# Twenty first-layer units ahead of pairs 8 and 9 in a fused attention and feed-forward kernel

## The chip, the cores and the metric

The kernel runs on one core of one Trainium2 chip. A core has TensorE (PE, matrix products into PSUM), VectorE (DVE), ScalarE (ACT), GpSimd (POOL) and SyncE (SP); SP here does nothing but issue DMAs, and POOL issues DMAs beside its copies. Each engine runs its instructions in the order of the program, and waits for other engines by semaphores. The metric is the device time of one execution in microseconds; the median of several executions counts.

## What is computed

Sliding-window attention with global rows, and behind it two dense layers with the activation h·cos(h):

```python
def _attn_ref(q, k, v, global_idx):            # (8, 8, 576, 64)
    scores = scale * np.matmul(q, k.transpose(0, 1, 3, 2))
    mask = np.abs(pos[:, None] - pos[None, :]) <= 32
    mask = mask | is_global[:, None] | is_global[None, :]
    attn = softmax(np.where(mask, scores, -1e9))
    return np.matmul(attn, v)
def _moe_ref(x, w_in, w_out):                  # (4608, 512), (512, 2048), (2048, 512)
    h = x @ w_in
    g = h * np.cos(h)
    return g @ w_out
```

The eight heads of a batch entry stand side by side in the 512 columns of x; 8 × 576 tokens give 4608 rows.

## The kernel before

**Attention** goes by pairs of heads: 32 pairs, four to a batch entry. A pair's 576 tokens are cut into 11 blocks of 56 queries; to each block belong 8 global columns and a window of 120 keys. The steps of one pair `pr`:

- `local_k`, `local_q` (lines 484 to 504): local keys and queries are copied into `kw[pr % 4]` and `qb[pr % 4]`. From pair 8 on they come from `kT` and `qT`, which a transposing DMA has filled, and the copies are DVE's (L491, L504). `globals_k`, `globals_q` (L468 to L473) put the global columns beside them, on POOL.
- `scores(pr, g)` for g = 0, 1, 2: up to four matmuls into an `st` tile (L514), exponential on ACT (L516), mask on DVE (L517). `st` tiles have the PSUM tag `s`, three buffers.
- `values`: 22 small matmuls into `pv` (L526), which has one buffer; then DVE sums, takes reciprocals and scales into `xn` (L531 to L537).
- `turn_x`: six transposes on PE (L549), and DVE copies into `xT` (L551, L552); with the last pair of a batch entry POOL puts the global tokens in place (L557).

**The layers** go by tiles of 512 tokens, nine in all. A first-layer unit is `mlp_in(t, f)`: four matmuls of 512 columns (L567) for one of 16 slices of the hidden width; `mlp_act` then has the cosine on ACT (L573) and the product g on DVE (L574). Its PSUM tile has the tag `h` (two buffers); while `spare` is set, units with f % 4 of 2 or 3 use tag `s`. A second-layer unit is `mlp_out(t, u)`: four matmuls (L584); after every fourth one a result of 128 × 512 is copied out of PSUM, alternately by DVE (L591) and ACT (L589), and SP sends it to memory (L593). There are 144 units of each kind. `one` takes the next first-layer unit if its tokens are there (`ready[0]`), `two` the next second-layer unit, up to a limit `outs_by` of 8 for each stage.

**The order** is written by hand, as strings of steps. FRONT runs pairs 0 to 7, with all that builds masks, global columns and the first values. Then stages s = 3 to 15 follow; stage s runs pairs 2s (letter `a`) and 2s + 1 (`z`) and copies the keys and queries of the next two (`kc qc`, `kd qd`). In the strings `sa0` is `scores` of the first pair, `pa` its `values`, `xa` its `turn_x`; `1` is a first-layer unit with its activation, `m` one without, `t` an activation that was left open, `2` a second-layer unit; `n` is a sum of squares of an `xn` on ACT (L603); `K` casts a half batch entry's inputs to fp16 by POOL's DMAs, and `G` does so behind a small copy which waits for the stage's `xn` (`gate`, L738), in stage 4 with the gathers of the second half's global rows; `B` has SP load transposed keys and queries and the values of two pairs (L272 to L318, L379), and from stage 4 on each stage ends with it. Stage 3 is the string MID, since pairs 6 and 7 are already in FRONT. Stages 4 and 5 have strings of their own; all later ones use ORDER. Stage 5 ends with `build_globals`, whose transposes (L453) wait for the gathers. Behind the last stage the rest of the units of both layers alternate.

Of the kernel before, what the change touches and what calls it, by code (L numbers as in the profile page):

```python
# [17 lines left out]
B, H, S, D = 8, 8, 576, 64  # L18
# [5 lines left out]
G = 8  # L24
# [10 lines left out]
C = G + QB  # L35
# [4 lines left out]

ORDER = "sa0 sa1 sa2 2 2 2 sz0 2 sz1 sz2 pa 1 1 2 xa pz G 1 1 2 xz n 1 1 2 kc qc 1 kd qd 2 1"

MID = "+ K6 1 1 1 1 n1 kc qc 1 1 kd qd 1 1 B5"

FOURTH = "sa0 sa1 sa2 m sz0 m sz1 sz2 t t pa 1 1 1 pz 1 xa 1 1 xz G 1 n2 kc qc 1 1 kd qd 1 1"

FIFTH = "sa0 sa1 sa2 m sz0 m sz1 sz2 t t pa 1 1 1 pz 1 xa 1 1 xz G 1 2 2 1 2 2 1 2 kc qc 2 2 2 2 n3 2 2 kd qd n 2 2 2 2 2 -"

FRONT = ("s0.0 s0.1 s0.2 k1 q1 C0 w0 s1.0 s1.1 s1.2 L2 p0 k2 q2 C1 w1 x0 s2.0 s2.1 s2.2 W0 p1 k3 q3 w2 x1 "
         "s3.0 s3.1 s3.2 L3 W1 g4 p2 k4 q4 C2 w3 x2 s4.0 s4.1 s4.2 g5 c4 K4 p3 k5 q5 w4 x3 s5.0 s5.1 s5.2 W2 W3 g6 p4 k6 q6 C3 w5 x4 n0 "  # L50
         "s6.0 s6.1 s6.2 g7 K5 p5 k7 q7 w6 x5 B4 s7.0 s7.1 s7.2 O p6 w7 x6 p7 x7")
OK_ALL = float(P * (B * NP * 2 * BP + B))


# [5 lines left out]
def dview(ap, offset, *dims):  # L60

    return bass.AP(ap.tensor, ap.offset + offset, [list(d) for d in dims])
# [134 lines left out]
def kernel(  # L197
# [53 lines left out]
    def cast_half(s, which):  # L251

        base = s * 4 * S * D
        for x in which:
            if x == "v":
                nc.gpsimd.dma_start(v16[s * 4 * S : (s + 1) * 4 * S].rearrange("(n r) d -> n (r d)", r=16),
                                    dview(v, base, (16 * D, 4 * S // 16), (1, 16 * D)))
            else:
                src, dst = {"k": (k, k16), "q": (q, q16)}[x]
                nc.gpsimd.dma_start(dst[s].rearrange("t (h d) -> t h d", h=4),  # L260
                                    dview(src, base, (D, S), (S * D, 4), (1, D)))
# [174 lines left out]
    def build_globals(half):  # L436
        both = []
        for src, dst in ((kg32, kgT), (qg32, qgT)):
            g16 = work.tile([P, P], FP16, tag="g16")
            nc.scalar.copy(g16, src[:, half].rearrange("x h d -> x (h d)"))  # L440
            both.append((g16, dst))
            if half == 0:
                turn_globals(half, both)
        turn_globals(half, both)

        if half:
            nc.scalar.copy(vg16[:, half], vg32[:, half])
# [111 lines left out]
    def mlp_in(t, f):  # L559
        if f == 0:  # L560
            g_of[t] = work.tile([P, NF, TT], FP16, tag="g", name="g")
        g16 = g_of[t]
        tag = "s" if spare[0] and f % 4 > 1 else "h"
        ph = ps.tile([P, TT], FP32, tag=tag, bufs={"s": 3, "h": 2}[tag], name="ph")
        ph_of.append((ph, g16[:, f]))
        for j in range(NC):
            nc.tensor.matmul(ph, w_in16[:, j, f * P : (f + 1) * P], xT[:, j, t * TT : (t + 1) * TT],  # L567
                             start=(j == 0), stop=(j == NC - 1))

    def mlp_act():  # L570
        ph, g = ph_of.pop(0)
        cos = work.tile([P, TT], FP16, tag="cos", bufs=3)
        nc.scalar.activation(cos, ph, AF.Sin, bias=pio2)  # L573
        nc.vector.tensor_tensor(g, cos, ph, ALU.mult)  # L574
# [24 lines left out]
    def x_squares(s):  # L599

        sq = work.tile([P, 2 * BP * P], FP16, tag="sq", bufs=1)
        xn = xn_of.pop(s)
        nc.scalar.activation(sq, view(xn, (1, 2 * BP * P)), AF.Square,  # L603
                             accum_out=x_sq[:, s : s + 1])
# [48 lines left out]
    def one(act=True):  # L653
        for _ in range(1):

            if ins_q and ins_q[0][0] < ready[0] and ins_q[0][0] < outs_q[0][0] + 2:
                t, f = ins_q.pop(0)
                mlp_in(t, f)
                if act:
                    mlp_act()  # L660
                ready[1] = t * NF + f + 1

    def two(n=1):
        for _ in range(n):
            t, u = outs_q[0] if outs_q else (NTT, 0)

            need = min(t * NF + 4 * (u % 4) + 7, (t + 1) * NF)
            if outs_q and need <= ready[1] and (tail[0] or NTT * NF - len(outs_q) < outs_by[0]):
                mlp_out(*outs_q.pop(0))

    outs_by = [0]
    ready = [0, 0]
# [11 lines left out]
    with tc.manual_schedule():  # L684
# [47 lines left out]
        def globals_kq(pr):  # L732
            globals_k(pr)
            globals_q(pr)

        def casts(s):

            nc.gpsimd.tensor_copy(gate, xn_of[s][0:1, 1, 0, 0:1])  # L738
            for n in range(6, 2 * B):
                if s == n - 3:  # L740
                    cast_half(n, "vkq")
            if s == 4:
                for src, dst in ((k, kg32), (q, qg32), (v, vg32)):
                    gather(src, dst, 1)

        def bring(s):

            turn_half(s)
            load_values(2 * s)
            load_values(2 * s + 1)  # L750

        LOCAL = {"k": local_k, "q": local_q}
        OTHER = LOCAL | {"g": globals_kq, "L": load_qk, "W": load_w_in, "c": lambda s: cast_half(s, "v"), "v": load_values, "n": x_squares,
                 "w": spread, "C": cast_vn, "V": hold, "O": load_w_out, "K": lambda s: cast_half(s, "kq" if s == 4 else "vkq"), "B": bring}
        for step in FRONT.split():
            f = (STEPS | OTHER)[step[0]]
            f(*[int(x) for x in (step[1:] or "0").split(".")])
# [2 lines left out]
        for s in range(3, B * NP // 2):  # L760
            outs_by[0] = 8 * (s - 3)
            for pr in (2 * s + 2, 2 * s + 3):
                if 8 <= pr < B * NP:
                    globals_kq(pr)
            for step in {3: MID, 4: FOURTH, 5: FIFTH}.get(s, ORDER).split():
                if step == "1":
                    one()
                elif step == "m":
                    one(False)
                elif step == "t":  # L770
                    mlp_act()
                elif step in "+-":
                    spare[0] = step == "+"
                elif step == "2":
                    two()
                elif step == "n":
                    x_squares(s - 1)
                elif step == "R":
                    ready[0] = 2
                elif step == "T":  # L780
                    bring(s + 2)
                elif step == "G":
                    casts(s)
                elif step[0] in "cvWCOVBSN" or step[1].isdigit():
                    (STEPS | OTHER)[step[0]](*[int(x) for x in (step[1:] or "0").split(".")])
                else:
                    f, pr = (STEPS | OTHER)[step[0]], 2 * s + "azcd".index(step[1])
                    if pr < B * NP:
                        f(pr, *[int(x) for x in step[2:]])
            if s % 2 == 1:  # L790
                ready[0] = s // 2 + 1 + (s // 2 == B - 1)
            if 3 < s < B * NP // 2 - 2:
                bring(s + 2)
            if s == 5:
                build_globals(1)
# [50 lines left out]
```

## Time and profile before

| | |
|---|---|
| median of 3 executions | 376.35 us (376.26 to 377.45) |
| the profiled execution | 376.97 us, of which the span from first to last instruction is 375.3 |
| busy, share of the span | PE 90%, DVE 71%, ACT 67%, POOL 29% |
| first layer on PE (L567), 576 matmuls | 141.8 us |
| second layer on PE (L584), 576 matmuls | 140.0 us |
| scores, values and transposes on PE (L514, L526, L549) | 30.2, 18.6 and 16.0 us |
| cosines on ACT (L573), 144 | 96.6 us |
| products g on DVE (L574), 144 | 96.0 us |

A line of a timeline has a start and a length in us, the engine, the line of the kernel, the operation with its output and inputs, and a count when like instructions are merged; in square brackets stands for how long the engine had been idle ahead of it, and what it waited for. A matmul's length includes the time in which it drains, so PE's rows overlap; the distance from start to start is what one costs in a row.

### The profile page before, as it was taken

The page shows a single profiled execution, that of the slowest core. Times are in us where ns is not written, and L with a number is a line of the kernel's source. Part 1 is how long each engine was busy: PE and PEld are TensorE (multiplying, and loading weights), DVE is VectorE, ACT ScalarE, POOL GpSimd, SP SyncE. Part 2 cuts the span into 40 slices and gives each one's busy share as a digit, 9 for nine tenths or more (in the row PEclk, how much of TensorE's full clock was granted, in tenths as well). Part 3 has the DMA queues.
Part 4 walks back from the last instruction along what each step waited for, and adds up shares of the span by engine and source line. Part 5 has one row for each costly group of instructions (what it writes and reads, how often), then busy time and mean ns, then how long its engine had stood idle before and what let it go on. Part 6 is the DMA issues. An engine that isn't in the chain of part 4 may idle for free.

```text
span 375.3 us, 7919 instructions
## 1 busy us (share of the span) xinstructions
PE 337.0 (90%) x2934; PEld 185.6 (49%) x2934; DVE 266.5 (71%) x615; ACT 249.7 (67%) x384; POOL 110.6 (29%) x244
## 2 busy tenths in 40 slices
PE   0399887679689999999999999999999999999993
PEld 0278775334344455555555555555555444444441
DVE  7648997959685288888889788888889454446410
ACT  5479795866944577686787777686787856654400
POOL 6635392805526032525071434413000200000000
PEclk9999999989999999999999999999999999999998
DMA  5989999999999599999999999999950000110021
GB/s 92 197 128 155 168 155 176 216 163 133 162 62 145 139 95 139 141 206 109 192 124 179 144 185 172 133 197 95 166 80 31 28 30 28 47 38 28 35 80 64
DMA packets 175320, 45.56 MB, mean 121 GB/s; under 512 B 163882, under 2 KB 170282, under 8 KB 175082
## 3 DMA queue, kind: packets, MB, share of 16 engines
q1 hardware_dynamic: 111449, 27.41, 55.0%
q0 software_dynamic: 63824, 17.57, 47.1%
q8 instruction: 25, 0.41, 0.5%
q14 instruction: 22, 0.17, 0.2%
HBM read 45.07 MB, written 20.05 MB: 174 GB/s over the span
## 4 chain that ended last, share of the span: by engine, by line
PE 75%; DVE 11%; ACT 4%; issue 4%; DMA 3%; POOL 2%; POOLq 0%; ACTq 0%; DVEq 0%
PE po L584 33%; PE ph L567 29%; PE st L514 5%; DVE g L574 3%; PE pv L526 3%; PE tx L549 2%; DVE xn L537 2%; DMA kn<-in_k_dram 2%; ACT e L516 1%; DMA vg<-in_v_dram,gidx_rows 1%; PE t L372 1%; ACT cos L573 1%; DVE pm L517 1%; PE pn L617 1%; ACT L573 1%
## 5 line engine op out<-in xcount | busy, mean ns | idle before, releaser
L573 ACT ACTIVATE cos<-ph,pio 128x512 f16<-128x512 f32 x144 | 96.6, 687 | 71.7 <-PE ph L567 71.4
L567 PE MATMUL ph<-xT,w_in 128*128 128x512 f16 x576 | 141.8, 382 | 2.6 <-DVE g L574 2.5
L584 PE MATMUL po<-w_out,g 128*128 128x512 f16 x576 | 140.0, 379 | 0.0
L574 DVE TENSOR_TENSOR g<-cos,ph 128x512 f16<-128x512 f16 x144 | 96.0, 685 | 50.6 <-ACT cos L573 48.6
L584 PEld LDWEIGHTS <-g 128*128 128x128 f16 x576 | 55.4, 98 | 63.0
L567 PEld LDWEIGHTS <-w_in 128*128 128x128 f16 x576 | 53.8, 98 | 62.2 <-issue 3.9
L516 ACT ACTIVATE e<-st 128x512 f16<-128x512 f32 (+1 forms) x96 | 48.1, 561 | 11.2 <-DVE pm L517 5.4
L517 DVE TENSOR_TENSOR pm<-e,mask 128x512 f16<-128x512 f16 (+1 forms) x96 | 37.0, 404 | 25.5 <-ACT e L516 23.9
L738 POOL COPY gate<-xn 1x1 f16<-1x1 f16 x12 | 2.2, 179 | 131.8 <-DVE xn L537 131.8
L514 PE MATMUL st<-qb,kw 128*128 128x128 f16 x352 | 30.2, 227 | 9.1 <-DVE g L574 5.0
L514 PEld LDWEIGHTS <-kw 128*128 128x128 f16 x352 | 25.0, 102 | 19.6 <-issue 10.4
L537 DVE TENSOR_TENSOR xn<-pv,r_all 128x768 f16<-128x768 f32 x32 | 30.7, 958 | 1.7
L260 POOL DMA_DIRECT2D q<-in_q_dram x12 | 25.9, 2161 | 0.0
L557 POOL COPY xT<-xg 128x4 f16 x64 | 17.8, 277 | 26.5 <-DVE xT L552 15.8
L589 ACT COPY o<-po 128x512 f32<-128x512 f32 x18 | 10.5, 586 | 21.3 <-PE po L584 21.0
L603 ACT ACTIVATE sq<-xn 128x1536 f16<-128x1536 f16 x16 | 23.6, 1476 | 0.0
L504 DVE COPY qb<-qT 64x616 f16<-64x616 f16 x48 | 22.1, 459 | 0.3
L526 PE MATMUL pv<-vw,pm 128*64 128x65 f16 x704 | 18.6, 198 | 2.4 <-DVE xn L537 2.0
L372 PE MATMUL t<-xT 112*128 112x128 f16 (+1 forms) x168 | 19.8, 230 | 0.7 <-ACT xT L347 0.4
L260 POOL DMA_DIRECT2D k<-in_k_dram x12 | 19.7, 1642 | 0.5 <-issue 0.5
L591 DVE COPY o<-po 128x512 f32<-128x512 f32 x18 | 12.3, 686 | 9.5 <-PE po L584 9.5
L549 PE MATMUL tx<-ident,xn 128*128 128x128 f16 x192 | 16.0, 219 | 2.8 <-DVE xn L537 1.8
(120 smaller groups left out, 333.3 us busy)
## 6 DMA issues: line engine op xcount, KB each, us to landing
out_dram<-o SPq DMA_DIRECT2D x36, 256.0 KB
vw<-v SPq DMA_DIRECT2D x35, 165.0 KB
v<-in_v_dram POOLq DMA_DIRECT2D x12, 288.0 KB, 5.8
k<-in_k_dram POOLq DMA_DIRECT2D x12, 288.0 KB, 8.7
q<-in_q_dram POOLq DMA_DIRECT2D x12, 288.0 KB, 11.3
vn<-in_v_dram SPq DMA_DIRECT2D x20, 112.0 KB
w_in<-in_moe_w_in_dram POOLq DMA_DIRECT2D x4, 512.0 KB, 9.1
w_out<-in_moe_w_out_dram POOLq DMA_DIRECT2D x1, 2048.0 KB, 23.2
```

The lines of the kernel that those rows point to most:

```text
L260: nc.gpsimd.dma_start(dst[s].rearrange("t (h d) -> t h d", h=4), dview(src, base, (D, S), (S * D, 4), (1, D)))
L372: nc.tensor.matmul(t[:, j - g0], shift[0:m, a], new[0:m, x, h0 : h0 + 2 * D], start=False, stop=(a, x) == parts[-1])
L514: nc.tensor.matmul(st[:, j], kp[:, g0 + j], view(qp[:, :, g0 + j], (NB * C, 2), (1, C)), start=True, stop=True)
L516: nc.scalar.activation(e[:, :n], st[:, :n], AF.Exp, scale=scale)
L517: nc.vector.tensor_tensor(view(pm[:, g0], (1, n * P)), view(e, (1, n * P)), view(mask[:, g0], (1, n * P)), ALU.mult)
L526: nc.tensor.matmul(pv[r0 : r0 + C, j // 6, c0 : c0 + 65], pm[:, j, h], vp[:, j, h], start=True, stop=True)
L537: nc.vector.tensor_tensor(view(xn, (384, 2), (D, 6), (1, D)), view(pv, (512, 2), (65, 6), (1, D)), view(rp, (6, 2), (1, 6), (0, D)), ALU.mult)
L567: nc.tensor.matmul(ph, w_in16[:, j, f * P : (f + 1) * P], xT[:, j, t * TT : (t + 1) * TT], start=(j == 0), stop=(j == NC - 1))
L573: nc.scalar.activation(cos, ph, AF.Sin, bias=pio2)
L574: nc.vector.tensor_tensor(g, cos, ph, ALU.mult)
L584: nc.tensor.matmul(po, g16[:, f, s * P : (s + 1) * P], w_out16[:, f], start=(f == 0), stop=(f == NF - 1))
L603: nc.scalar.activation(sq, view(xn, (1, 2 * BP * P)), AF.Square, accum_out=x_sq[:, s : s + 1])
```

## The change

Only the order strings change, and two letters of FRONT are new.

```diff
-MID = "+ K6 1 1 1 1 n1 kc qc 1 1 kd qd 1 1 B5"
-
-FOURTH = "sa0 sa1 sa2 m sz0 m sz1 sz2 t t pa 1 1 1 pz 1 xa 1 1 xz G 1 n2 kc qc 1 1 kd qd 1 1"
-
-FIFTH = "sa0 sa1 sa2 m sz0 m sz1 sz2 t t pa 1 1 1 pz 1 xa 1 1 xz G 1 2 2 1 2 2 1 2 kc qc 2 2 2 2 n3 2 2 kd qd n 2 2 2 2 2 -"
+MID = "+ K6 1 1 kc qc 1 1 1 1 kd qd 1 1 1 1 B5 1 1 n2 1 1 1 1 1 1 -"
+
+FIFTH = "sa0 sa1 sa2 2 2 sz0 2 sz1 sz2 2 pa 1 2 xa pz G 1 2 xz n 1 2 kc qc 1 kd qd 2"
...
-         "s6.0 s6.1 s6.2 g7 K5 p5 k7 q7 w6 x5 B4 s7.0 s7.1 s7.2 O p6 w7 x6 p7 x7")
+         "s6.0 s6.1 s6.2 g7 K5 p5 k7 q7 w6 x5 B4 s7.0 s7.1 s7.2 O p6 w7 n1 x6 m p7 m x7 t t")
...
+                 ... "m": lambda _: one(False), "t": lambda _: mlp_act()}
+        ready[0] = 1
...
-            for step in {3: MID, 4: FOURTH, 5: FIFTH}.get(s, ORDER).split():
+            for step in {3: MID, 5: FIFTH}.get(s, ORDER).split():
```

The string of the stages that now cover pairs 8 and 9 too, unchanged:

```python
ORDER = "sa0 sa1 sa2 2 2 2 sz0 2 sz1 sz2 pa 1 1 2 xa pz G 1 1 2 xz n 1 1 2 kc qc 1 kd qd 2 1"
```

Counted out, first-layer units before are 8 in MID, 13 in stage 4 and 11 in stage 5, and second-layer units 16, all in stage 5. Now 2 first-layer units stand at the end of FRONT, 18 in MID, 8 in stage 4 and 4 in stage 5; second-layer units are 8 in each of stages 4 and 5. Spare is set through MID alone, where it had lasted to the end of stage 5. The squares n1 move into FRONT and n2 into MID.

ScalarE, from the last copy of values for pair 7 to the table load for pair 8's exponentials, before (`vw` values, `cos` the cosines, `sq` squares of `xn`):

```order
L375 CAST vw_94<-t 128x6x64
L573 ACT_TABLE_LOAD
L573 ACTIVATE cos<-ph,pio_71 128x512 x4
L603 ACTIVATE sq,x_sq<-xn 128x1536
L573 ACTIVATE cos<-ph,pio_71 128x512 x4
L516 ACT_TABLE_LOAD
```

and now, where all lines behind the strings stand one or two lower:

```order
L373 CAST vw_94<-t 128x6x64
L601 ACTIVATE sq,x_sq<-xn 128x1536
L571 ACT_TABLE_LOAD
L571 ACTIVATE cos<-ph,pio_71 128x512 x14
L601 ACTIVATE sq,x_sq<-xn 128x1536
L571 ACTIVATE cos<-ph,pio_71 128x512 x6
L514 ACT_TABLE_LOAD
```

Twenty cosines stand there in place of eight, the first squares come ahead of them and a second sum of squares is ahead of the last six.

VectorE in the same stretch, from the end of FRONT to the first mask of pair 8, before (`g` the products, `kw` and `qb` keys and queries of pairs 8 and 9, `pm` the masked exponentials):

```order
L759 MEMSET ones_121 128x128
L574 TENSOR_TENSOR g<-cos,ph 128x512 x4
L491 COPY kw_95<-kT_83 128x11x120
L504 COPY qb_99<-qT_85 64x11x56 x2
L574 TENSOR_TENSOR g<-cos,ph 128x512 x2
L491 COPY kw_96<-kT_83 128x11x120
L504 COPY qb_100<-qT_85 64x11x56 x2
L574 TENSOR_TENSOR g<-cos,ph 128x512 x2
L517 TENSOR_TENSOR pm<-e,mask 128x512 x2
```

and now:

```order
L572 TENSOR_TENSOR g<-cos,ph 128x512 x2
L758 MEMSET ones_121 128x128
L572 TENSOR_TENSOR g<-cos,ph 128x512 x2
L489 COPY kw_95<-kT_83 128x11x120
L502 COPY qb_99<-qT_85 64x11x56 x2
L572 TENSOR_TENSOR g<-cos,ph 128x512 x4
L489 COPY kw_96<-kT_83 128x11x120
L502 COPY qb_100<-qT_85 64x11x56 x2
L572 TENSOR_TENSOR g<-cos,ph 128x512 x12
L515 TENSOR_TENSOR pm<-e,mask 128x512 x2
```

Both groups of copies keep their place by the count of products ahead of them, within two; behind them stand twelve products instead of two.

VectorE in stage 5, from the masks of pairs 10 and 11 to the transposed `xn` of pair 10 (`o` an output copied from PSUM, `dg` and `r_all` the softmax sums), before:

```order
L517 TENSOR_TENSOR pm<-e,mask 128x512 x2
L517 TENSOR_TENSOR pm<-e,mask 128x384
L574 TENSOR_TENSOR g<-cos,ph 128x512 x2
L531 TENSOR_REDUCE dg<-pv 8x2
L532 RECIPROCAL r_all<-pv 128x12
L533 RECIPROCAL r_all<-dg 8x12
L537 TENSOR_TENSOR xn<-pv,r_all 128x768
L574 TENSOR_TENSOR g<-cos,ph 128x512 x3
```

and now:

```order
L515 TENSOR_TENSOR pm<-e,mask 128x512 x2
L515 TENSOR_TENSOR pm<-e,mask 128x384
L589 COPY o<-po 128x512
L529 TENSOR_REDUCE dg<-pv 8x2
L530 RECIPROCAL r_all<-pv 128x12
L531 RECIPROCAL r_all<-dg 8x12
L535 TENSOR_TENSOR xn<-pv,r_all 128x768
L572 TENSOR_TENSOR g<-cos,ph 128x512
```

The two products ahead of the softmax sums became one copy of an output, and behind `xn` one product stands in place of three.

More of the change, by code (lines that the diff above doesn't have):

```diff
@@ L753 @@
         OTHER = LOCAL | {"g": globals_kq, "L": load_qk, "W": load_w_in, "c": lambda s: cast_half(s, "v"), "v": load_values, "n": x_squares,
-                 "w": spread, "C": cast_vn, "V": hold, "O": load_w_out, "K": lambda s: cast_half(s, "kq" if s == 4 else "vkq"), "B": bring}
+                 "w": spread, "C": cast_vn, "V": hold, "O": load_w_out, "K": lambda s: cast_half(s, "kq" if s == 4 else "vkq"), "B": bring, "m": lambda _: one(False), "t": lambda _: mlp_act()}
+        ready[0] = 1
         for step in FRONT.split():
```

## The prediction

> **What bounds the kernel now.** I read the page's 40 slices first, then TensorE's timeline around the stages that the change touches, then the vector and scalar engines beside it.
>
> ```profile
> PE   0399887679689999999999999999999999999993
> PEclk9999999989999999999999999999999999999998
> ```
>
> A slice is 9.4 us. From the 13th slice (113 us) on TensorE shows 9 until the last slice; from the 5th slice to the 12th it shows 6 to 8 (9 once), and in the ninth its granted clock falls as well. So there are two regimes. The later one is seen in two repeats of a stage in windows of TensorE's timeline (columns: length; busy us of PE, PEld, DVE, ACT, POOL; clock; DMA share; GB/s):
>
> ```profile
> 143.51:160.43 16.92, 16.92 (x143) 9.06 (x142) 14.54 (x34) 12.92 (x19) 5.47 (x12) 1.00 1.50 137
> 160.43:177.35 16.92, 16.92 (x143) 9.07 (x142) 14.49 (x34) 12.92 (x19) 7.22 (x17) 1.00 1.34 159
> ```
>
> A stage by ORDER is two pairs of attention, eight first-layer units ("ins") and eight second-layer units ("outs"); TensorE never stops in it, while DVE keeps 2.4 us free. The earlier regime, in TensorE's timeline (start, length; in brackets the idle time before a row and what ended it):
>
> ```profile
> 63.72 0.51 PE L549 MATMUL tx<-ident,xn 128*128 128x128 f16 x6 [1.65 <-DVE xn L537]
> 64.06 7.07 PE L567 MATMUL ph<-xT,w_in 128*128 128x512 f16 x32
> 70.97 0.39 PE L514 MATMUL st<-qb,kw 128*128 128x128 f16 x4
> 74.25 0.55 PE L514 MATMUL st<-qb,kw 128*128 128x128 f16 x7 [2.89 <-DVE g L574]
> ...
> 82.38 1.02 PE L567 MATMUL ph<-xT,w_in 128*128 128x512 f16 x4 [1.24 <-DVE g L574]
> 84.43 0.54 PE L526 MATMUL pv<-vw,pm 128*64 128x65 f16 x22 [1.02 <-DVE xn L537]
> ...
> 88.77 0.51 PE L549 MATMUL tx<-ident,xn 128*128 128x128 f16 x6 [0.77 <-DVE xT L552]
> ...
> 94.28 0.38 PE L514 MATMUL st<-qb,kw 128*128 128x128 f16 x4 [0.46 <-DVE g L574]
> 96.30 0.33 PE L514 MATMUL st<-qb,kw 128*128 128x128 f16 x3 [1.64 <-DVE g L574]
> ...
> 102.59 1.02 PE L567 MATMUL ph<-xT,w_in 128*128 128x512 f16 x4 [1.22 <-DVE g L574]
> 104.64 0.54 PE L526 MATMUL pv<-vw,pm 128*64 128x65 f16 x22 [1.03 <-DVE xn L537]
> ...
> 114.84 10.52 PE L584 MATMUL po<-w_out,g 128*128 128x512 f16 x48
> 126.24 0.43 PE L453 MATMUL t<-ident,g 128*128 128x128 f16 x2 [0.88 <-ACT g L440]
> 126.54 0.84 PE L514 MATMUL st<-qb,kw 128*128 128x128 f16 x11
> ```
>
> From the first unit at 64.06 to the first score of pair 12 at 126.54 pass 62.48 us, with 11.15 us of idle in the rows shown. TensorE has only ins to put between the steps of pairs 8 to 11, and every in needs ACT and DVE afterwards, the engines that attention waits for; meanwhile the outs, which need neither but for one copy in four, are saved up and run in a block at 114.84. One stall costs twice, by the clock (windows, as above):
>
> ```profile
> 74.00:76.00 2.00, 1.75 (x13) 1.00 (x13) 1.83 (x5) 1.07 (x3) 0.03 (x1) 0.79 1.68 267
> 76.00:78.00 2.00, 2.00 (x10) 0.90 (x8) 0.46 (x2) 0.60 (x1) 0.00 (x0) 0.50 1.24 130
> 78.00:80.00 2.00, 2.00 (x34) 1.50 (x33) 0.74 (x2) 1.35 (x3) 0.00 (x0) 0.86 1.71 142
> ```
>
> Half clock for about 0.84 + 2.00 + 0.56 = 3.4 us (0.79 and 0.86 of 2 us are mixtures of 1 and 0.5) loses some 1.7 us.
>
> **The change, part by part.** Work is only moved: by the end of pair 11 both kernels have issued 32 ins and 16 outs, and from pair 12 on the order is the same. So I compute when pair 12's first score starts and carry the difference to the end.
>
> A unit: eight in 70.97 − 64.06 = 6.91 us, 0.864 us each. A stage's attention: 16.92 − 16 × 0.864 = 3.10 us of TensorE.
>
> *Front.* Unit 1 stands after x6, in the 1.65 us gap at 63.72; pair 7's values, their DVE chain and x7 move 0.86 us back, and unit 2 fits into the rest of the gap. The later units start at 64.06 + 0.86 = 64.92 with two done.
>
> *TensorE's own work* from there: 46 units × 0.864 = 39.74, two stages of attention 6.20, the two transposes of L453 0.30 (126.24 to 126.54): 46.24 us, so 111.16 without a stall. The stalls that I expect:
>
> *First stage, 18 ins.* DVE's rows of before:
>
> ```profile
> 69.05 0.53 DVE L491 COPY kw<-kT 128x1320 f16<-128x1320 f16 x1
> 69.49 0.93 DVE L504 COPY qb<-qT 64x616 f16<-64x616 f16 x2
> 70.48 1.29 DVE L574 TENSOR_TENSOR g<-cos,ph 128x512 f16<-128x512 f16 x2
> 71.68 0.94 DVE L491 COPY kw<-kT 128x1320 f16<-128x1320 f16 x1
> 72.55 0.93 DVE L504 COPY qb<-qT 64x616 f16<-64x616 f16 x2
> 73.51 1.29 DVE L574 TENSOR_TENSOR g<-cos,ph 128x512 f16<-128x512 f16 x2
> ```
>
> A product g costs DVE 0.60 us in a row (two from 70.48 to 71.68), less than TensorE's 0.864, so the ins alone are TensorE's. The copies of K and Q for one pair cost 1.43 (69.05 to 70.48) or 1.83 (71.68 to 73.51). I take 1.83 for both, as GpSimd will be copying global columns then; with 1.43 the stall below is about 0.8 shorter. [...] DVE's order is now 4 g, copies, 4 g, copies, 12 g (with a short memset). Units with f % 4 of 0 and 1 have two PSUM tiles: such a unit waits for the g of four units before. With ACT's table load and first two cosines ending near 65.6, DVE ends g of f = 4 at 70.45 and of f = 8 at 74.7; unit 8 would start at 70.1 and unit 12 at 73.9. Stalls 0.4 + 0.8.
>
> *End of that stage.* ACT's rows:
>
> ```profile
> 68.31 1.47 ACT L603 ACTIVATE sq<-xn 128x1536 f16<-128x1536 f16 x1
> ...
> 69.77 2.41 ACT L573 ACTIVATE cos<-ph,pio 128x512 f16<-128x512 f32 x4
> ```
>
> The squares n2 (1.46 to the next start) stand ahead of the last six cosines (0.60 each): the last cosine ends at 82.3 and the last g at 82.9, against a last unit at 81.7. Scores need those tiles: pair 8's third group waits 0.75 us. Ending with ins leaves this wait, but of the 2.89 before it is the small remainder, since no copies are queued behind.
>
> *Pairs 8 and 9* run by ORDER: 16.92 us, no stall, as in the windows above.
>
> *Pairs 10 and 11* run by the new FIFTH: 12 units, 10.37 + 3.10 = 13.47. In a stage by ORDER the first masked exponentials start 2.83 us after the scores:
>
> ```profile
> 146.34 1.23 DVE L517 TENSOR_TENSOR pm<-e,mask 128x512 f16<-128x512 f16 x3 [0.59 <-ACT e L516]
> ```
>
> (146.34 − 143.51). The next pair's scores reuse the tile which that exponential frees; ORDER has three outs ahead of them, FIFTH two: 0.67 + 1.73 = 2.4, a wait of 0.4. Between pv and the transposes FIFTH has two units where ORDER has three, while the xn chain behind an output copy needs over 1.7: another 0.5. Together 0.9; bounds 0 (as ORDER) and 2.3 (1.24 + 1.02 at 82.38 and 84.43, the old order's).
>
> *Transposes of L453*: the 0.88 wait for ACT stays, 0.9.
>
> Stalls 0.4 + 0.8 + 0.75 + 0.9 + 0.9 = 3.75, and pair 12 starts at 111.16 + 3.75 = 114.9, against 126.54: **11.6 us earlier**. What goes is most of 11.15 us of idle, the 1.7 of the clock, and the time in which matmuls drained at each stall.
>
> *What moves forward with it.* Three loads lose cover. Their rows (GpSimd's timeline, the table of DMA issues):
>
> ```profile
> 55.49 2.24 POOL L681 DMA_DIRECT2D w_out<-in_moe_w_out_dram  x1
> w_out<-in_moe_w_out_dram POOLq DMA_DIRECT2D x1, 2048.0 KB, 23.2
> 87.68 0.18 POOL L738 COPY gate<-xn 1x1 f16<-1x1 f16 x1 [13.65 <-DVE xn L537]
> 103.37 0.26 POOL L473 COPY qb<-qgT 64x88 f16<-64x88 f16 x1 [3.36 <-DMA vg<-in_v_dram,gidx_rows]
> ```
>
> w_out lands at 55.49 + 23.2 = 78.7; the first out, at 109.66 before, now comes at about 83.1: 4.4 us to spare. The gathers of the second half's globals hold GpSimd from the gate until 15.7 us later; the gate now comes near 93, so they end near 109, and pair 12's columns and L453's inputs are due at 114. The K and Q transposes of pairs 12 and 13 begin with stage 4's end and are used some 12 us later. All hidden, at 0; without cover each costs its lateness.
>
> **Sum.** The profiled execution took 376.97 us (span 375.3): 376.97 − 11.6 = 365.4. The median of the runs shown, 376.35, lies 0.6 lower, so the predicted median is **364.8 us**.
>
> **The rivals.**
>
> *A. The alternation does not fill the waits in its first stages* (0.17). If pairs 8 to 11 keep the old stalls of 82.38 to 104.64 that wait for xn or a cosine, two stages lose about 2.3 each where I count 0.9 in one: 3.7 more, 368.5. For it: DVE enters these stages late by a queue of g. Against: in five ORDER stages no stall.
>
> *B. w_out comes late* (0.07). It shares the DMA engines with casts and value loads; 2 to 5 us beyond its margin gives 367 to 370. Against: nothing that stands ahead of it in the queues is changed.
>
> *C. The half clock stays* (0.05). In the windows the clock fell after 2.89 us of idle, and did not fall after the 1.24 + 1.02 at 82.38 and 84.43. If it falls again after shorter stalls, 1.7 us come back: 366.5. [...]
>
> *D. SyncE's queue becomes the bound: slower* (0.05). Its timeline:
>
> ```profile
> 114.90 11.45 SPq L593 DMA_DIRECT2D out_dram<-o  x4
> 126.44 1.34 SPq L272 DMA_TRANSPOSE kT<-k  x1
> ...
> 194.68 2.08 SPq L272 DMA_TRANSPOSE kT<-k  x1
> ...
> 213.65 3.07 SPq L272 DMA_TRANSPOSE kT<-k  x1
> ...
> 262.52 1.41 SPq L272 DMA_TRANSPOSE kT<-k  x1
> ```
>
> Before, SyncE sat waiting for outputs until 126 and entered the long regime with an empty queue; now it enters it straight from the loads of pairs 10 to 13. One stage's loads can take 213.65 − 194.68 = 18.97 us against TensorE's 16.92. If all ten stages with loads did, the lag would be 20.5 us, of which about 8 are free (an estimate: the transposes are issued in the first 6 us and used some 14 us in): 12.5 us lost, 377.9. It decides against the change from 1.96 us of lag per stage on. Against it: from 126.44 to 262.52 eight stages took 17.01 each, TensorE's own pace. A lag just under that cancels the gain: no difference (0.03).
>
> **How the numbers follow.** Forecast 0.63, with a range of its own from 362 (nearly all 3.75 us of stalls gone) to 366.5. A, B and C stretch it to 368.5; D and the far end of B are left out. Range 362.0 to 368.5. Faster by over 0.3% (about what a measurement of this kernel can tell from no change): 0.63 + 0.17 + 0.07 + 0.05 = 0.92; same 0.03; slower 0.05.
>
> **What the changed profile would show.** Two matmul groups of L567 around x7 near 62 and 63 us. L567 in a row from 65 to 82 with waits for g L574 of about a microsecond in all; a wait under 1 us at pair 8's scores; no clock under 1.0 between 70 and 120. L584 between the steps of pairs 8 and 9, no waits for xn there. Pair 12's first score near 115. From there every stage again 16.92 us. It is wrong if TensorE waits for w_out, a gather or kT; if stage 4 is over 18 us or stage 5 over 16; or if stages after pair 12 become longer than 17.

## The result

| | before | changed |
|---|---|---|
| median | 376.4 us (376.26 to 377.45, 4 executions) | 367.29 us (366.44 to 369.15, 4 executions) |
| profiled execution, span | 376.97, 375.3 | 366.44, 364.7 |
| busy share: PE, DVE, ACT, POOL | 90, 71, 67, 29% | 92, 74, 68, 30% |

The ratio is 0.976, with the interval 0.972 to 0.980: faster by about 9 us, inside the range on record and 2.5 us over the predicted median. In three later batches the ratio of the changed kernel was 0.977, 0.971 and 0.970. Ratios leave out executions that took over 1.5% longer than the fastest of their kernel; medians and ranges take all. (In the changed kernel every line behind the order strings stands one or two lower than before: units of the first layer are L565, of the second L582, scores L512, products g L572, key copies L489.)

The page's slices of TensorE after the change, the row of its clock below:

```profile
PE   0399988989998999999999999999999999999992
PEclk9999999999999999999999999999999999999997
```

The sixes and sevens between the fifth and the twelfth slice are gone, and so is the fall of the clock in the ninth. The windows of the changed stretch (columns as in the prediction): from the transposes of pair 6 (x6) to the first score of pair 8, on to that of pair 10, on to that of pair 12, and the rest:

```profile
59.90:81.02 21.12, 19.04 (x114) 8.80 (x115) 18.02 (x34) 16.95 (x25) 8.39 (x23) 1.00 1.63 186
81.02:99.15 18.13, 17.24 (x143) 9.14 (x142) 13.90 (x32) 13.02 (x20) 5.22 (x6) 1.00 1.26 117
99.15:115.85 16.70, 14.39 (x130) 7.34 (x129) 14.14 (x31) 12.28 (x22) 11.09 (x20) 1.00 1.42 147
115.85:364.70 248.85, 242.26 (x1758) 123.54 (x1758) 174.95 (x384) 163.72 (x246) 52.45 (x131) 0.99 0.98 112
```

From x6 to pair 12's first score pass 115.85 − 59.90 = 55.95 us; before they were 126.54 − 61.07 = 65.47. That is 9.52 us, and the 248.85 behind it were 375.3 − 126.54 = 248.76. So the whole gain lies in this stretch. The two profiled executions differ by 1.0 more, because x6 itself came 1.2 earlier; that is scatter of the front, where the profiles of all kernels below put x6 anywhere between 59.67 and 62.43.

TensorE's timeline after, with all its waits in the stretch but two of 0.44 and 0.17:

```profile
60.25 1.03 PE L565 MATMUL ph<-xT,w_in 128*128 128x512 f16 x4
...
61.70 1.04 PE L565 MATMUL ph<-xT,w_in 128*128 128x512 f16 x4
63.41 0.51 PE L547 MATMUL tx<-ident,xn 128*128 128x128 f16 x6 [0.67 <-DVE xn L535]
63.75 9.01 PE L565 MATMUL ph<-xT,w_in 128*128 128x512 f16 x40
74.12 7.07 PE L565 MATMUL ph<-xT,w_in 128*128 128x512 f16 x32 [1.35 <-DVE g L572]
81.02 0.39 PE L512 MATMUL st<-qb,kw 128*128 128x128 f16 x4
81.94 0.38 PE L512 MATMUL st<-qb,kw 128*128 128x128 f16 x4 [0.53 <-DVE g L572]
82.68 0.33 PE L512 MATMUL st<-qb,kw 128*128 128x128 f16 x3 [0.36 <-DVE g L572]
82.85 2.75 PE L582 MATMUL po<-w_out,g 128*128 128x512 f16 x12
...
114.59 0.43 PE L451 MATMUL t<-ident,g 128*128 128x128 f16 x2 [0.88 <-ACT g L438]
115.85 0.78 PE L512 MATMUL st<-qb,kw 128*128 128x128 f16 x11 [0.83 <-POOL xT L555]
```

From x6 on, 13.06 us of idle stood in brackets before, and 5.23 are left. Inside stage 4 (82.85 to 99.15) there is none. The last wait is new. Its row names a POOL copy, but the cause is read from what DVE and POOL did just then. DVE's timeline:

```profile
70.81 1.68 DVE L489 COPY kw<-kT 128x1320 f16<-128x1320 f16 x1
...
112.49 2.41 DVE L489 COPY kw<-kT 128x1320 f16<-128x1320 f16 x1
114.81 0.93 DVE L502 COPY qb<-qT 64x616 f16<-64x616 f16 x2
```

POOL's:

```profile
69.94 2.20 POOL L258 DMA_DIRECT2D q<-in_q_dram  x1
...
109.39 0.26 POOL L471 COPY qb<-qgT 64x88 f16<-64x88 f16 x1 [3.97 <-DMA vg<-in_v_dram,gidx_rows]
...
110.54 0.18 POOL L736 COPY gate<-xn 1x1 f16<-1x1 f16 x1
...
111.21 1.70 POOL L258 DMA_DIRECT2D k<-in_k_dram  x1
112.32 2.21 POOL L258 DMA_DIRECT2D q<-in_q_dram  x1
```

The key copy of 0.53 us takes 1.68 and 2.41 where POOL is issuing the q cast, and ends 0.35 and 0.37 behind that instruction: 70.81 + 1.68 = 72.49 against 69.94 + 2.20 = 72.14; 114.90 against 114.53. The query copies behind it end near 115.7, and pair 12's first score starts at 115.85.

### The profile page after: what moved, and what is told of

Its sections match the earlier page's. It is cut to its first block, busy times and chain, and to the rows that moved or that the text cites. A ratio compares the mean times of both kernels' runs of the same rounds, so it can differ in the third digit from the quotient of the medians.

```text
span 364.7 us, 7918 instructions
## 1 busy us (share of the span) xinstructions
PE 335.0 (92%) x2934; PEld 184.1 (50%) x2934; DVE 268.4 (74%) x615; ACT 249.8 (68%) x384; POOL 110.6 (30%) x244
## 4 chain that ended last, share of the span: by engine, by line
PE 80%; DVE 6%; ACT 3%; DMA 3%; POOL 3%; issue 2%; POOLq 0%; ACTq 0%
PE po L582 32%; PE ph L565 31%; PE st L512 5%; PE pv L524 4%; PE tx L547 3%; PE t L370 2%; DVE g L572 2%; DMA kn<-in_k_dram 2%; ACT e L514 1%; DMA vg<-in_v_dram,gidx_rows 1%; PE t L366 1%; DVE xn L535 1%; PE pn L615 1%; POOL xT L555 1%; ACT cos L571 1%
## 5 line engine op out<-in xcount | busy, mean ns | idle before, releaser
L582 PE MATMUL po<-w_out,g 128*128 128x512 f16 x576 | 141.6, 379 | 0.0
L565 PE MATMUL ph<-xT,w_in 128*128 128x512 f16 x576 | 140.1, 379 | 1.5 <-DVE g L572 1.4
L572 DVE TENSOR_TENSOR g<-cos,ph 128x512 f16<-128x512 f16 x144 | 95.9, 685 | 46.5 <-ACT cos L571 44.3
L582 PEld LDWEIGHTS <-g 128*128 128x128 f16 x576 | 55.2, 98 | 61.8
L565 PEld LDWEIGHTS <-w_in 128*128 128x128 f16 x576 | 53.7, 98 | 61.8 <-issue 2.3
L512 PE MATMUL st<-qb,kw 128*128 128x128 f16 x352 | 29.3, 224 | 5.9 <-POOL qb L471 2.8
L512 PEld LDWEIGHTS <-kw 128*128 128x128 f16 x352 | 24.2, 100 | 16.3 <-issue 5.5
L555 POOL COPY xT<-xg 128x4 f16 x64 | 19.2, 300 | 20.6 <-DVE xT L550 17.2
L366 PE MATMUL t<-vg,xT 128*128 128x128 f16 x88 | 17.1, 232 | 0.1
```

What stands on the lines that cost most here:

```text
L512: nc.tensor.matmul(st[:, j], kp[:, g0 + j], view(qp[:, :, g0 + j], (NB * C, 2), (1, C)), start=True, stop=True)
L582: nc.tensor.matmul(po, g16[:, f, s * P : (s + 1) * P], w_out16[:, f], start=(f == 0), stop=(f == NF - 1))
```

## The experiments

Executions scatter by more than these variants differ, so each is read in two ways: by its median beside the changed kernel in the same batch, and by two distances in TensorE's timeline of its profile, from x6 to pair 10's first score and from there to pair 12's. The first distance repeats well: the changed kernel shows 39.24 to 39.26 in all four of its profiles. The second does not, which is told below.

| kernel | median (range) | x6 to pair 10 | pair 10 to 12 | sum |
|---|---|---|---|---|
| changed, first | 367.29 (366.44–369.15) | 39.25 | 16.70 | 55.95 |
| a1_again | 369.65 (368.64–371.69) | 39.26 | 19.72 | 58.98 |
| e1_gate_late | 371.2 (369.42–371.51) | 39.25 | 19.39 | 58.64 |
| e2_no_front | 370.25 (369.05–371.95) | 39.66 | 19.27 | 58.93 |
| e4_copies_late | 368.88 (367.29–371.01, and one of 1200.92) | 37.98 | 19.23 | 57.21 |
| a2_again | 367.45 (365.39–372.89) | 39.25 | 15.74 | 54.99 |
| e3_sixteen | 366.2 (365.13–369.46) | 36.02 | 18.34 | 54.36 |
| e5_ins_only | 382.26 (380.23–383.82) | 38.92 | 30.75 | 69.67 |
| e6_gathers_early | 365.92 (365.29–367.6) | 39.27 | 15.75 | 55.02 |
| a3_again | 367.95 (366.52–370.78) | 39.24 | 15.74 | 54.98 |
| e6_second | 369.13 (365.39–371.7) | 39.27 | 15.76 | 55.03 |
| e7_all | 368.36 (366.74–371.96) | 36.35 | 18.34 | 54.69 |
| e8_gathers_back | 368.65 (366.44–375.26) | 34.63 | 20.81 | 55.44 |

e1, e2 and e4 ran in a1's batch, e3, e5 and e6 in a2's, e6_second and e7 in a3's; e8 ran beside the kernel before only. e3, e7 and e8 have four units, 3.46 us, less in the first distance and more in the second; e5 has ten units less in the first and ten more in the second.

### The changed kernel three more times

> The changed kernel once more, beside the variants below. My theory: 366.4 to 367.4 us, and in an execution whose mean granted clock is 0.990 rather than 0.995 about 1.7 us more, because one half-clock window then falls on busy matmuls near the end of the 18 units. Rival: the spread of 366.44 to 369.15 comes from DMA and shows no tie to the clock.

> The changed kernel once more, beside the next three: about 369 us, as in the runs beside the first experiments (366.4 to 371.7 so far). Both theories of those runs expect the same here; it is the yardstick.

> The changed kernel as the yardstick of the next two: 367.3 to 369.7, the medians so far. If an exponential of pair 11 stands 2.5 to 3.4 us with its scores ready, as in the first experiments, 369 or more; without that, as beside the second ones, near 367.3.

The yardsticks gave 369.65, 367.45 and 367.95. The first expectation missed: a1 lies 2.3 us above its upper end. Its executions do go with the clock (371.69 at a granted clock of 0.986, 368.64 at 0.996), but the half clock of its profile is not near the end of the 18 units, where eight of them take 83.56 − 76.66 = 6.90 us, as in the first profile (81.02 − 74.12); it comes in stage 5. The condition of the third expectation is what the profiles show: a1, with 369 or more, is the one in which an exponential of pair 11 stands, ScalarE's timeline:

```profile
108.83 0.98 ACT L514 ACTIVATE e<-st 128x512 f16<-128x512 f32 x2 [2.98 <-remote]
```

and TensorE's:

```profile
108.06 0.19 PE L524 MATMUL pv<-vw,pm 128*64 128x65 f16 x1 [0.50 <-issue]
108.77 0.24 PE L524 MATMUL pv<-vw,pm 128*64 128x65 f16 x2 [0.51 <-issue]
...
110.86 1.87 PE L582 MATMUL po<-w_out,g 128*128 128x512 f16 x4 [0.88 <-DVE o L589]
```

Both engines stop within 2 us of each other for nothing that the profile shows, and the second distance grows from 15.74 to 19.72. In the windows behind it the clock has fallen too:

```profile
110.00:112.00 2.00, 1.15 (x3) 0.41 (x3) 1.93 (x6) 1.80 (x2) 0.00 (x0) 0.71 1.45 102
112.00:114.00 2.00, 2.00 (x30) 1.39 (x28) 1.43 (x4) 0.00 (x0) 0.98 (x4) 0.50 0.97 73
114.00:116.00 2.00, 2.00 (x15) 0.94 (x12) 1.52 (x5) 0.77 (x2) 0.18 (x1) 0.94 0.86 47
```

In a2 and a3 nothing of this is seen, and the new wait ahead of pair 12 is not there either. There the gathers landed later, so the casts came later against the copies (in a2 the gate opens 52.3 us behind x6, in the first profile 50.6), and it was pair 13's key copy that they met, which nothing waits for so closely. a2's DVE timeline:

```profile
114.31 0.53 DVE L489 COPY kw<-kT 128x1320 f16<-128x1320 f16 x1
...
116.32 2.22 DVE L489 COPY kw<-kT 128x1320 f16<-128x1320 f16 x1
```

So this wait costs 16.70 − 15.74 = 0.96 us in some executions, not in all.

### The casts of stage 5 behind the transposes of pair 11

```diff
-FIFTH = "... pa 1 2 xa pz G 1 2 xz n 1 2 kc qc 1 kd qd 2"
+FIFTH = "... pa 1 2 xa pz 1 2 xz G n 1 2 kc qc 1 kd qd 2"
```

> In the order of pairs 10 and 11 the casts (G) come behind the transposes of pair 11, so GpSimd copies the global tokens first and issues the casts about 2 us later. My theory: the copy of pair 12's keys at 112.49 took 2.41 us because GpSimd was issuing the q cast (112.32 to 114.53) at that moment; now it takes under 1 us, pair 12's first score no longer waits 0.83 us, and the time falls by 0.8 us to about 366.4. Rival (the wait is for GpSimd's copies into xT, which the profile names as the releaser): these end earlier here too, but the key copy stays long whenever any GpSimd work is beside it, and the wait stays at 0.5 us or more: 367.0 to 367.3.

Pair 12's key copy took 0.56 us, but the casts met the next one. DVE's timeline:

```profile
116.23 0.56 DVE L489 COPY kw<-kT 128x1320 f16<-128x1320 f16 x1
...
118.28 3.22 DVE L489 COPY kw<-kT 128x1320 f16<-128x1320 f16 x1
```

TensorE's:

```profile
122.45 0.38 PE L512 MATMUL st<-qb,kw 128*128 128x128 f16 x4 [0.40 <-POOL kw L466]
```

The wait moved to pair 13, and the median, expected 0.8 us lower, is 1.5 us above a1's. The collision is confirmed, the remedy is not one.

### Without the two units and the squares in FRONT

```diff
-MID = "+ K6 1 1 kc qc 1 1 1 1 kd qd 1 1 1 1 B5 1 1 n2 1 1 1 1 1 1 -"
+MID = "+ K6 1 1 1 1 kc qc 1 1 1 1 kd qd 1 1 1 1 B5 n1 1 1 n2 1 1 1 1 1 1 -"
...
-         "... O p6 w7 n1 x6 m p7 m x7 t t")
+         "... O p6 w7 x6 p7 x7")
```

> The two units and the squares n1 go back from the end of FRONT into the first stage (20 units there); all else is as in the changed kernel. My theory: the gap of 1.65 us between pair 7's values and its transposes opens again and holds no unit: 0.87 us more, 368.1. Rival (the two early units only shift work, since DVE is what the 18 units end on): no difference, 367.3.

TensorE's timeline:

```profile
62.33 0.51 PE L547 MATMUL tx<-ident,xn 128*128 128x128 f16 x6 [1.65 <-DVE xn L535]
62.68 10.74 PE L565 MATMUL ph<-xT,w_in 128*128 128x512 f16 x48
73.71 7.18 PE L565 MATMUL ph<-xT,w_in 128*128 128x512 f16 x32 [0.29 <-DVE g L572]
```

The old gap of 1.65 is back, but the wait for g falls from 1.35 to 0.29, 1.06 less. That is what pair 9's key copy has become shorter, from 1.68 to 0.62: counted from x6 it begins 0.9 us later here, and the issue of the q cast is over 1.0 us sooner, ahead of it. DVE's row and POOL's:

```profile
71.47 0.62 DVE L489 COPY kw<-kT 128x1320 f16<-128x1320 f16 x1
```

```profile
68.83 2.05 POOL L258 DMA_DIRECT2D q<-in_q_dram  x1
```

The first distance grows by 0.41 and the median by 0.6, between the theory's 0.87 and the rival's nothing. The distance is a balance. Up to pair 8's first score (80.73) the version without the two units is 0.06 ahead: the shorter copy pays for the open gap; then pair 8's scores wait for g 1.14 and 0.21 instead of 0.53 and 0.36, with the squares n1 now among that stage's cosines. What the two units are worth by themselves isn't shown.

### Pair 9's copies four units later

```diff
-MID = "+ K6 1 1 kc qc 1 1 1 1 kd qd 1 1 1 1 B5 ...
+MID = "+ K6 1 1 kc qc 1 1 1 1 1 1 1 1 kd qd B5 ...
```

> In the first stage the copies of pair 9's keys and queries come four units later. My theory: the 1.35 us wait of the unit at 74.12 comes from the key copy of 1.68 us at 70.81, which stood beside GpSimd's q cast (69.94 to 72.14); four units later that cast is over, the copy takes 0.5 to 0.9 us, the wait is under 0.4 us, and the time falls by about 1.0 us to 366.2. Rival (VectorE simply has too much to do in the stage, 20 products and six copies): the wait moves to a later unit or to pair 8's scores and the time stays within 0.3 us of 367.3.

```profile
63.95 16.16 PE L565 MATMUL ph<-xT,w_in 128*128 128x512 f16 x72
79.94 0.39 PE L512 MATMUL st<-qb,kw 128*128 128x128 f16 x4
80.74 0.38 PE L512 MATMUL st<-qb,kw 128*128 128x128 f16 x4 [0.41 <-DVE g L572]
81.60 0.33 PE L512 MATMUL st<-qb,kw 128*128 128x128 f16 x3 [0.48 <-DVE g L572]
```

In TensorE's timeline all eighteen units run in one row. Pair 9's key copy takes 0.53 here, as at the same place in e7 (75.98) and e8 (74.74), so the wait of 1.35 was made by the long copy, and it does not return behind it: the waits at pair 8's scores are together as long as before, 0.41 and 0.48. The first distance is 1.27 shorter, the median 0.8 lower (1.9 without the execution that took 1200.92).

### Sixteen units ahead, stage 5 by ORDER

```diff
-MID = "+ K6 1 1 kc qc 1 1 1 1 kd qd 1 1 1 1 B5 1 1 n2 1 1 1 1 1 1 -"
+MID = "+ K6 1 1 kc qc 1 1 1 1 kd qd 1 1 B5 1 1 n2 1 1 1 1 -"
...
-            for step in {3: MID, 5: FIFTH}.get(s, ORDER).split():
+            for step in {3: MID}.get(s, ORDER).split():
```

> Sixteen units ahead instead of twenty; the fourth and the fifth stage then both run by ORDER, and pair 12 starts with the same work done. Theory 'the cast issue behind the gathers holds the key copy of pair 12': the gate of the fourth stage opens 3.5 us sooner before pair 12 than now, the gathers land before the fifth stage's end, the key copy ahead of pair 12 takes 0.5 us again and the 0.8 at its first score goes; with the 0.44 wait for an exponential in FIFTH gone too, 1.5 to 2 us faster than the changed kernel beside it. Rival 'all work is only moved and TensorE is full': no difference, within 0.5 us. Rival 'the stock of twenty is needed': the outs of the fourth and fifth stage wait for g, 1 us or more slower.

No out waits for a g, so a stock of twenty isn't needed. The wait of 0.44 for an exponential is gone; the key copy ahead of pair 12 still takes 1.75 (it ends 0.35 behind the q cast), but pair 12's score no longer waits for POOL. The sum of the distances is 0.63 below a2's. The medians lie 1.3 apart with ranges that overlap, so a gain in time is not shown, and no run tried a stock of less than sixteen.

### Twenty ahead, but no outs beside pairs 8 to 11

```diff
-MID = "... 1 1 n2 1 1 1 1 1 1 -"
+MID = "... 1 1 n2 1 1 1 1 1 1"
+FOURTH = "sa0 sa1 sa2 m sz0 m sz1 sz2 t t pa 1 pz xa 1 xz G 1 n kc qc 1 kd qd"
+FIFTH = "sa0 sa1 sa2 m sz0 m sz1 sz2 t t pa 1 pz xa 1 xz G 1 n kc qc 1 kd qd 2 2 2 2 2 2 2 2 2 2 2 2 2 2 2 2 -"
...
-            for step in {3: MID, 5: FIFTH}.get(s, ORDER).split():
+            for step in {3: MID, 4: FOURTH, 5: FIFTH}.get(s, ORDER).split():
```

> Twenty units ahead as in the change, but pairs 8 to 11 then get six first-layer units each stage and no outs; the sixteen outs stand in a block ahead of pair 12, as in the kernel before. Theory 'the alternation with outs fills the waits of attention': the idle time of the fourth and fifth stage of the kernel before (5.9 us in 22.46 and some 4.4 in 13.57) comes back, 8 to 10 us slower than the changed kernel, about 377. Rival 'it is enough that units run ahead, and fewer units beside attention leave DVE and ACT free': at most 2 us slower.

14.8 us slower than the changed kernel beside it, more than the 8 to 10 expected, and slower than the kernel before (ratio 1.013, interval 1.006 to 1.019). TensorE's timeline, the two longest waits:

```profile
92.08 0.54 PE L526 MATMUL pv<-vw,pm 128*64 128x65 f16 x22 [4.20 <-DVE xn L537]
...
110.21 0.82 PE L526 MATMUL pv<-vw,pm 128*64 128x65 f16 x22 [3.88 <-DVE xn L537]
```

and the windows around their ends, where the clock falls each time:

```profile
92.00:94.00 2.00, 1.92 (x31) 1.33 (x31) 1.88 (x6) 0.00 (x0) 0.00 (x0) 0.66 1.17 93
110.00:112.00 2.00, 1.79 (x29) 1.45 (x29) 1.61 (x6) 0.00 (x0) 0.00 (x0) 0.50 1.20 60
```

With the same units ahead and the same work done before pair 12, the gain is gone. It comes from outs standing between the steps of attention, with the units ahead as their stock. The clock adds to the loss: at 0.66 and 0.50, these two windows alone lack 2.00 × (0.34 + 0.50) = 1.7 us of full clock (an estimate). So does another difference: spare lasts to the end of stage 5 here, as in the kernel before, and a unit waits 1.11 us at 101.51 for a score tile, until its exponential has run. How much of the 14.8 us belongs to each isn't separated.

### The gathers early, twice

```diff
-MID = "... kd qd 1 1 1 1 B5 ...
+MID = "... kd qd N 1 1 1 1 B5 ...
...
-            if s == 4:
-                for src, dst in ((k, kg32), (q, qg32), (v, vg32)): gather(src, dst, 1)
...
+            nc.gpsimd.tensor_copy(gate, qb[9 % NK][0:1, 0, 0, G : G + 1])
+            for src, dst in ((k, kg32), (q, qg32), (v, vg32)): gather(src, dst, 1)
```

> The six gathers of the second half's globals move on GpSimd from behind the casts of the fourth stage (97.5 to 105) to some 20 us sooner, behind the key copies of pair 9, where GpSimd is idle. Theory 'the casts come late because GpSimd is held until the gathers land': the next gate opens at its tile's readiness, some 2 us sooner, the key copy ahead of pair 12 takes 0.5 instead of 2.4 us, and the wait of 0.8 at pair 12's first score goes: 0.8 to 1.1 us faster than the changed kernel beside it; if the exponentials of pair 11 also stop waiting 2.5 to 3.4 us in the fifth stage, as they do in the runs of the first experiments, those waits are tied to the gathers and it is 2 to 4 us faster. Rival 'the wait only moves': within 0.5 us, with the long key copy at pair 13 or the stall of the fifth stage at another place.

> The gathers on GpSimd some 20 us sooner, a second time: beside the last run of the changed kernel the medians differed by 1.5 us, but pair 12's first score came equally long after the transposes of pair 6 (55.0 us in both), so the order alone explained nothing of it. Theory 'the casts are held by the gathers, and that costs 0.8 in some executions only': 0 to 0.9 us faster here, the key copy ahead of pair 12 at most 1.5 us, no wait at its first score. Theory 'the stall of an exponential of pair 11 hangs on the gathers beside it': where the changed kernel shows that stall, this one does not, and is 2 to 4 us faster. Rival 'nothing but scatter': within 0.5 us.

Against a2 and a3 the distances are the same (15.75 and 15.76 to 15.74), the medians once 1.5 lower and once 1.2 higher, and the ratios to the kernel before 0.970 and 0.964 against 0.971 and 0.970, with intervals that overlap. So no gain is shown, and none comes from this stretch. Freed of the gathers, the gate waits for its `xn` until 109.61, 0.9 before the 110.54 above instead of 2, so the casts meet the key copy nevertheless (1.49 us in both), and no score waits. The stall of the exponential wasn't there in either, but not in a2 and a3 either, so this pair tells nothing of it.

### All together, and the same without the early gathers

```diff
-MID = "+ K6 1 1 kc qc 1 1 1 1 kd qd 1 1 1 1 B5 1 1 n2 1 1 1 1 1 1 -"
+MID = "+ K6 1 1 kc qc 1 1 1 1 1 1 1 1 kd qd N B5 1 1 1 1 -"
+FOURTH = "sa0 sa1 sa2 2 2 2 sz0 2 sz1 sz2 pa 1 1 2 xa n2 pz G 1 1 2 xz n 1 1 2 kc qc 1 kd qd 2 1"
...
-            for step in {3: MID, 5: FIFTH}.get(s, ORDER).split():
+            for step in {3: MID, 4: FOURTH}.get(s, ORDER).split():
```

with the gathers moved as in the version above, and for the second version `N` taken out, with the gathers back behind the casts of stage 4.

> Sixteen units ahead, the fourth and fifth stage in the order of the later ones, pair 9's key and query copies four units later, the squares of pairs 4 and 5 moved into the fourth stage where ScalarE idles, and the gathers early. Theory 'each wait left in the changed kernel has its own cause, and they add': the 1.4 us in the units ahead, most of the 0.9 at pair 8's scores, the 0.4 for an exponential and the 0.8 ahead of pair 12 go: 2 to 3 us faster than the changed kernel beside it, pair 12's first score about 52.5 us after the transposes of pair 6 instead of 55 to 56. Rival 'the waits move': at most 1 us faster, with new waits for g at the outs of pairs 8 and 9 or for pair 9's copies.

> The last version without its early gathers: sixteen units ahead, both later stages in the order of the rest, pair 9's copies four units later, the squares of pairs 4 and 5 in the fourth stage, and the gathers behind the casts as in the change. Theory 'a key copy that meets the issue of the casts is what moves from place to place, and the early gathers pushed the casts of the fourth stage onto pair 10's key copy': pair 10's key copy takes 0.53 instead of 2.66 us, the wait of 1.5 at its first score goes, and pair 12's first score comes 52.9 to 53.6 us after the transposes of pair 6 (54.7 in the last version, 55 to 56 in the changed kernel): 1.5 to 3 us faster than the changed kernel, 364.5 to 366.5 where the front end of the execution does not lose the clock. Rival 'these waits hang on the scatter of the executions, not on the order': the wait at pair 10's first score comes again, or one as long at pair 12's.

In e7 pair 12's first score comes 54.69 us behind x6 instead of 52.5, and the median is 0.4 above a3's: the waits moved, as the rival says. The gathers made the casts of stage 4 late, and they met pair 10's key copy. DVE's row, POOL's, and TensorE's, each from its timeline:

```profile
94.48 2.66 DVE L491 COPY kw<-kT 128x1320 f16<-128x1320 f16 x1
```

```profile
94.57 2.21 POOL L260 DMA_DIRECT2D q<-in_q_dram  x1
```

```profile
98.10 0.77 PE L514 MATMUL st<-qb,kw 128*128 128x128 f16 x11 [1.52 <-POOL kw L468]
```

With the gathers back (e8) that copy took 0.52, the wait went, and the first distance fell from 36.35 to 34.63: this half of the expectation held, to 0.2. But TensorE's timeline of the next stage:

```profile
100.92 0.27 PE L526 MATMUL pv<-vw,pm 128*64 128x65 f16 x4 [0.49 <-issue]
102.34 1.89 PE L567 MATMUL ph<-xT,w_in 128*128 128x512 f16 x8 [1.15 <-issue]
```

This is a1's kind of stall again. The stage took 20.81 − 18.34 = 2.47 us more than in e7, against the 1.72 that had been won, so the sum of 55.44 misses the 52.9 to 53.6 expected, and the median of 368.65 the 364.5 to 366.5. Neither version is shown to beat the changed kernel.

## Why the prediction came out so

By its own steps, on the distance from x6, against the first profile of the changed kernel:

| step | predicted | measured |
|---|---|---|
| front: x6 to x7, one unit added | +0.86 | 63.41 − 59.90 = 3.51 against 2.65: +0.86 |
| first stage's stalls (f = 8, f = 12) | 0.4 + 0.8 | none, and one of 1.35 that takes 1.73 from row to row |
| pair 8's scores wait for g | 0.75 | 0.53 + 0.36, 1.21 by the stage's length (18.13 − 16.92) |
| stage 4 otherwise | 16.92, no stall | 16.92, no stall |
| stage 5 with L451 | 13.47 + 0.9 + 0.9 + 0.30 = 15.57 | 16.70; 15.74 without the new wait |
| from pair 12 on | as before | 248.85 against 248.76 |

The **mechanism was right**: the ins run ahead at TensorE's pace (the last eight in 81.02 − 74.12 = 6.90 us), alternation fills stage 4 from its first out, and the clock stays at 1.0 there; from its first out stage 4 takes 16.30 (82.85 to 99.15), and a later stage of the kernel before took the same (144.13 to 160.43). e5 shows that without the outs the gain is lost. The miss on this distance is 55.95 − (114.9 − 61.07) = 2.1 us: 0.5, 0.5 and 1.1. Two of the prediction's own signs of being wrong were met, though the time lies in its range: stage 4 took 18.13 where 18 was the limit, and stage 5 16.70 where it was 16.

The **sizes of the stalls**: 0.5 in the first stage and 0.5 at its end. In the first stage the copies' length was read wrongly. I took 1.83 for both pairs 'as GpSimd will be copying global columns'; one took 1.41 (67.00 to 68.41), the other 2.57 (70.81 to 73.38). No run shows that reason: with GpSimd's copies of global columns beside it (66.84 and 67.15) the first key copy took its 0.53, while the second, of 1.68, met the issue of a cast. The row of before that I quoted shows such a meeting too: the copy at 71.68 ended at 72.62, 0.35 behind a cast. Together they took 0.32 more than forecast, and the first four products, with the memset, ended some 0.15 later behind x6. At the stage's end it is the last cosines and products, ScalarE's row and DVE's:

```profile
78.09 3.81 ACT L571 ACTIVATE cos<-ph,pio 128x512 f16<-128x512 f32 x6
```

```profile
78.80 3.83 DVE L572 TENSOR_TENSOR g<-cos,ph 128x512 f16<-128x512 f16 x6 [1.35 <-ACT cos L571]
```

Six cosines took 3.81 where I had counted 3.60, and the last product ended at 82.63, 0.73 behind the last cosine instead of 0.6. (A bracket is not a loss: the wait of 1.35 counts from 63.75 + 9.01 = 72.76, the end of the row before, where ten units of 0.864 would have started the next one at 72.39; from row to row 74.12 − 72.39 = 1.73 were lost.)

The **step that failed** is 'All hidden, at 0'. Its times came out, the gate at 93.25 for 'near 93' and the gathers' landing at 109.39 for 'near 109', in part by luck: counted from x6, which came 1.2 early, both are some 1.5 later than forecast. But I listed only who waits for POOL's *data* (pair 12's columns and L451), not who is held by POOL's *instructions*: the casts queued behind the gathers ran into DVE's key copy. It cost 0.96 there and nothing in a2 and a3.

From this 2.1 to the 2.5 us of the medians nothing is a step of the change: x6 came 1.2 earlier in the profile, which hid as much of the miss, the median is 0.85 above that profile, and 0.6 had been taken off for the median of before.

The **rivals**. A (old stalls in the first stages) is out: no such wait in stage 4. B (w_out late): no wait at 82.85. C (half clock) did not come in the first profile, but did in a1, at 110.8 (0.71 and 0.50 in its windows), and seems to have in the variant e1, where an out at 108.69 takes 1.87 us, as at 110.86 in a1, for the usual 1.03, both behind stalls that the prediction didn't know. D (SyncE's queue) left one trace in four profiles of the changed kernel; a3's TensorE timeline:

```profile
143.90 0.22 PE L524 MATMUL pv<-vw,pm 128*64 128x65 f16 x1 [1.78 <-DMA vw<-vg]
```

A value load came late once; that stage took 152.89 − 133.63 = 19.26, 2.3 us more than its neighbours. The other stages kept their pace, so the queue is not the bound.

**Open** is the stall without a releaser in stage 5. Of the nine profiles in which the gathers are issued in that stage beside outs, five have it (a1, e1, e2, e4, e8), and it starts within some 3 us of the last gather; the three with early gathers don't. The four of the first batch (a1, e1, e2, e4) all have it. The record names the chip, too: these four ran on chip 13 and e8 on chip 2, while a2, a3 and e3, without it, ran on chip 15 (for the first profile no chip is named). So the chip, or something else that a batch has in common, may matter as much as the gathers; no run separated these.

## What to carry to other kernels

When attention's chains leave TensorE idle, give it work that hardly needs another engine, and run the other layer's units early just far enough to have that work in stock: sixteen were as good as twenty here (366.2 us beside 367.45). When a step is moved, list for each instruction that it issues, DMA issues too, not only who waits for its result but which copies of other engines run beside it. Measure a stall's price by the distance of rows, not by its bracket (1.73 against 1.35 above).

## What the hardware showed unexpectedly

- **A key copy on DVE ended 0.35 to 0.37 us behind GpSimd's cast issue.** In 19 meetings between 70 and 122 us the copy of 0.53 us took 0.82 to 3.22: 0.94 and 0.99 before; 1.68 and 2.41 in the first profile after; 1.84 in a1; 1.68 and 2.22 in a2; 1.68 and 2.67 in a3; 3.22 in e1; 1.90 in e2; 1.69 and 1.75 in e3; 1.90 in e4; 1.49 in e6; 1.68 and 1.49 in e6_second; 2.66 in e7; 0.82 in e8. Each ended 0.35 to 0.37 behind the end of the q cast, also when only the k cast was being issued as it began (a3 at 116.27, e1, e7). Two copies that began 0.07 and 0.17 us behind the start of a k or a v cast took 0.53 all the same (before at 69.05, a2 at 114.31). What makes the difference, no run shows.
- **Idle time alone didn't tell when the clock fell.** In a1 a window at half clock followed brackets of 0.50, 0.51 and 0.88 us within 3.5 us; in e4 brackets of 0.69, 0.53 and 0.86 at the same place did not slow the matmuls: the out behind them, at 107.59, takes 1.02, the one in a1, at 110.86, 1.87. The stretch at half clock was 3.4 us long in a1 (1.16 + 2.00 + 0.24, an estimate from the 0.71, 0.50 and 0.94 of its three windows).
- **Two engines stand together with no wait on record**, in some executions only: ScalarE for 2.50 to 3.38 us (a1, e1, e2, e4), and TensorE, in the same four and in e8, in brackets of 0.49 to 1.29; see the open point.
